# Two bias units moved behind the second half step's scores, and first-layer weight operations entered in the engine sharing

## The chip, the cores and the metric

The program runs on one core of one Trainium2 chip. The metric is the device time of an execution in microseconds; the kernel before takes 644.47 us (median of 3 runs, 644.24 to 644.6).

## The reference

An attention layer with a computed bias feeds two gated feed-forward layers, all float32:

```python
scores = scale * np.matmul(q, k.transpose(0, 1, 3, 2))          # B 2, H 8, S 576, D 64
x = (log1p(abs(i - j)) / log1p(max(i, 1)))[..., None]
bias = np.maximum(x @ w1 + b1, 0.0) @ w2                        # 32 hidden, 8 heads
attn = softmax(scores + bias)
x = np.matmul(attn, v)                                          # 1152 tokens, 512 wide
x = (x @ w_a) * (x @ w_b) @ w_out                               # 512 -> 1536 -> 512
x = (silu(x @ w_gate) * (x @ w_val)) @ w_out2
```

## The kernel before

Attention is done in half steps. A step is one pair of heads and one tile of rows; the first four steps (`t` 4) have one half each, the other sixteen have two (one per batch), 36 halves in all. The main loop (line 474) runs a pipeline over them: iteration i issues `first(i)` (scores on the tensor engine PE into the one PSUM tile `ps`, then, on the vector engine DVE, two row minima with the bias added, line 339, and, on the scalar engine ACT, two exponentials, line 345), `second(i - 1)` (nine transposes of the exponentials `es` on PE in three groups, each into a PSUM bank `tp` that is copied out as `ee`, lines 350 and 352) and `third(i - 2)` (values: `pu` from `ee` and `vv`). Every second half (and each of the first four) also transposes the inverse sums `rw` and copies them out as `rc`. There is one `ps` tile, so the scores of a half start after the minima of the half before; there are three `tp` banks, so a group of transposes waits until an earlier bank has been copied out.

The bias is made in between, in 36 units of 16 rows. `passes(u)` computes four tiles `hd` (lines 154 on DVE, 156 on ACT; eight buffers, two units' worth), and `products(u)` multiplies them on PE into one or two `tp` banks, copies these out scaled as `bt` (lines 160 and 162, the widths tell the units apart: unit 5 is 496 wide, 6 is 480, 7 is 464, 8 is 448, 9 is 432) and writes `bt` to DRAM (`bias_d`, on SP's queue). The rows of a step are read back from there by POOL's queue; those of half 4, the first of tile 0, need units 0 to 7. Four units are made ahead of the loop (`FIRST`), the rest in numbers given by `MADE`: 8 in iteration 0, 2 and 1 in turn after it. In iteration 0 the scores stand behind the fifth of these eight (`SCORED`), the minima behind the eighth, and those minima are held in program order on DVE.

PE's matmuls are all held in program order (line 100 is the helper `Pinned`, which records them; all of them have its line). What is not held is ordered by a scheduler. Work that either engine can do (`hd`, `bt`, `ee`, `rc`, `qa`, `ka`) is given to the one with less work so far, by two running sums, `share.spent`, for DVE and ACT: `on_dve` adds a linear cost in the width and picks the smaller sum. From iteration 22 on, one operation an iteration of preparing the first layer's weights (lines 270 to 274, 284, 285: twelve operations of 1024 columns, nine on DVE, three on ACT) is issued beside attention; these were not entered in the sums.

The layers after attention are bound by PE's matmuls and are not touched.

Of the kernel before, what the change touches and what calls it, by code (L numbers as in the profile page):

```python
# [32 lines left out]

UNITS = (*range(32, 36), *range(32))
FIRST = 4
MADE = (8, *(2, 1) * 8)
SCORED = 4
HDS, BTS, EES = 8, 6, 4

# [12 lines left out]
@with_exitstack  # L52
def attention_moe_moe(ctx: ExitStack, tc: tile.TileContext, qd, kd, vd, cst, lm, wm1, wm2, out):
    dram = ctx.enter_context(tc.tile_pool(name="dram", bufs=1, space=DRAM))
    bias_d = [dram.tile([P if t < 4 else 64, H, BW], F32, name=f"bias_d{t}") for t in range(5)]
    wpa = ctx.enter_context(tc.tile_pool(name="wpa", bufs=1))
    ident = wpa.tile([P, P], F32, name="ident")
    make_identity(tc.nc, ident)
    xpool = ctx.enter_context(tc.tile_pool(name="xpool", bufs=1))
    weights = Weights(tc, (wm1, wm2))  # L60
    x = Activations(xpool)

    with (
        tc.tile_pool(name="prep", bufs=2) as prep,
        tc.tile_pool(name="a4", bufs=3) as a4,
    ):
        share = Share()
        bias = ExitStack()
        staged = bias.enter_context(tc.tile_pool(name="staged", bufs=1, side="right"))
        heads = Heads(tc, prep, staged, qd, kd, vd, share)  # L70
        units = Bias(tc, bias, cst, lm, bias_d, heads, share)
        attention(ctx, tc, a4, heads, share, bias, units, bias_d, x, weights, ident)
    moe(tc, x, weights, out)
# [228 lines left out]
def attention(ctx, tc, a4, heads, share, bias, units, bias_d, x, weights, ident):  # L302
# [3 lines left out]
    with (  # L306
# [6 lines left out]
        def bias_rows(p, t, n):  # L313
            e = bias_d[t][:, 2 * p]
            return bass.AP(tensor=e.tensor, offset=e.offset + 15, ap=[[16 * H * BW, n // 16], [H * BW - 1, 16], [1, BW + S]])

        def scores(p, q, blocks, bt, sums):

            ka, kb = heads.got["k", p]
            qa, qb = q  # L320
            ps = ps2.tile([P, 2, 2, 512], F32, tag="big", name="ps")
            es = a4.tile([P, 2, S], F32, tag="es", name="es", bufs=3)
            for hf in range(2):
                for m, (lt, rt) in enumerate(((qa, ka), (qa, kb), (qb, ka))):
                    for j in range(2):
                        r = slice(64 * j, 64 * j + 64)
                        for n, (c0, b) in enumerate(blocks):
                            k0 = S * b + 288 * hf
                            pe.matmul(
                                ps[:, j, hf, :288], lt[r, c0 : c0 + P], rt[r, k0 : k0 + 288], start=m + n == 0, stop=m + n == len(blocks) + 1  # L330
                            )
            return ps, es, bt, sums

        def exponentials(ps, es, bt, sums, pinned):

            for j in range(2):
                nm = a4.tile([P, 1], F32, tag="nm", name="nm", bufs=4)
                least = (units.dve if pinned else nc.vector).tensor_tensor_reduce
                least(  # L339
                    out=es[:, j].rearrange("p (a j) -> p a j", a=2), in0=ps[:, j, :, :288], in1=bt[j].rearrange("p (a j) -> p a j", a=2),  # L340
                    op0=ALU.add, op1=ALU.min, scale=-0.125, scalar=3.0e38, accum_out=nm,
                )
                share.dve(S, 1.3)
                share.act(S, 190.0)
                nc.scalar.activation(es[:, j], es[:, j], AF.Exp, bias=nm, scale=-1.0, accum_out=sums[:, j : j + 1])  # L345
            return es.rearrange("p h k -> p (h k)")
# [81 lines left out]
        def first(i):  # L428

            idx, p, t, b = halves[i]  # L430
            if b == 0:
                bt = a4.tile([P, BW + S], F32, tag="bias", name="bt", bufs=3)
                for r in range(1 if t < 4 else B):
                    n = P if t < 4 else 64
                    heads.queue.dma_start(bt[n * r : n * r + n], bias_rows(p, t, n))
                bt = [bt[:, BW * j : BW * j + S] for j in range(2)]
                if 0 < idx < 3:
                    heads.load_v(idx + 1, nc.sync)
                    heads.split_k(idx + 1)
                if 6 <= idx + 2 < len(steps):  # L440
                    heads.fetch_q(*steps[idx + 2])
                cells[idx] = bt, a2.tile([P, 4 if t < 4 else 2], F32, tag=f"sums{t < 4}", name="sums", bufs=3)
            bt, sums = cells[idx]
            blocks = [(P * b, b)] if t < 4 else [(64 * r, r) for r in range(B)]
            for made in range(MADE[0] if i == 0 else 1):
                if i == 0:
                    units.products(*units.passes(rest.pop(0)), bank)
                if made == SCORED * (i == 0):
                    live[i] = scores(p, heads.got["q", p, t], blocks, bt, sums[:, 2 * b : 2 * b + 2])
            live[i] = exponentials(*live[i], i == 0)  # L450
            if idx == 2:
                heads.split_q(*steps[4])
            if 4 <= idx < len(steps) - 1 and b == 0:
                heads.split_q(*steps[idx + 1])

        def second(i):

            idx, p, t, b = halves[i]
            live[i] = transposed(live[i])
            if t == 4 or b == 1:  # L460
                cells["rc", idx] = inverses(place(t)[1], cells.pop(idx)[1])

        def third(i):

            idx, p, t, b = halves[i]
            if b == 0:
                cells["pu", idx] = ps0.tile([P, 512], F32, tag="pu", name="pu")
            pu = cells["pu", idx]
            blocks = [(slice(0, P), b, P * b)] if t < 4 else [(slice(64 * r, 64 * r + 64), r, 64 * r) for r in range(B)]
            values(p, pu, live.pop(i), blocks)  # L470
            if t == 4 or b == 1:
                finish(p, *place(t), cells.pop(("pu", idx)), cells.pop(("rc", idx)))

        for i in range(len(halves) + 2):
            todo = [units.passes(rest.pop(0)) for _ in range(MADE[i] if 0 < i < len(MADE) else 0)]
            if i < len(halves):
                first(i)
            if 0 <= i - 1 < len(halves):
                second(i - 1)
            if i >= 2:  # L480
                third(i - 2)
            for unit in todo:
                units.products(*unit, bank)
            if i == len(MADE) - 1:
                bias.close()
                weights.pool = weights.pools[0] = ctx.enter_context(tc.tile_pool(name="wpa2", bufs=1, side="right"))
                weights.fetch(0, 0, 0)
                weights.fetch(0, 0, 1)
                ahead = chain(weights.words(0, 0, 0), weights.split(0, 0, 0), weights.words(0, 0, 1))
            if i > len(MADE) + 4:  # L490
                for op in islice(ahead, 1):
                    units.tc.keep_in_program_order(op)


def place(t):
# [227 lines left out]
```

## Time and profile before

| | |
|---|---|
| median of 3 runs | 644.47 us (644.24 to 644.6) |
| the profiled execution | 645.35 us, its span 643.5 us |
| busy share of the span | PE 94%, DVE 83%, ACT 54%, POOL 7% |
| attention (to the first matmul of the first layer) | 0 to 200.17 us |
| mean granted TensorE clock | 0.995 |

The span runs from the first to the last instruction; the execution's time lies 1.85 us above it. The granted clock of PE is given as a share of 2.4 GHz; 0.5 is 1.2 GHz. A timeline row gives start, duration, engine, line, operation, the tiles, and in brackets the idle time of the engine before it and what ended that.

### The profile page before, as it was taken

To read this page: it belongs to the slowest core of one execution; us is meant where nothing else is said; L and a number is where in the kernel's file an instruction comes from. 1 tells how busy PE (TensorE), PEld (TensorE's weight loads), DVE (VectorE), ACT (ScalarE), POOL (GpSimd) and SP (SyncE) were. 2 spreads that over 40 slices of the span, in tenths; PEclk is the share of its full clock that TensorE was granted. 3 is DMA by queue.
4 is the path that set the end of the run, shared out by engine and by line. 5 is a ranking of instruction groups with operands and counts; after the bars stand their busy time and mean duration, and the time that the engine had idled before them with its cause. 6 is when DMAs were issued, how large, how long until landed. Compare 5 with 4: busy or idle time off the path is not lost.

```text
span 643.5 us, 11334 instructions
## 1 busy us (share of the span) xinstructions
PE 606.4 (94%) x4470; PEld 553.4 (86%) x4470; DVE 535.0 (83%) x1034; ACT 346.2 (54%) x673; POOL 45.6 (7%) x66
## 2 busy tenths in 40 slices
PE   4689898999899989999999999999989999999997
PEld 2266565688778989999999999899989999999997
DVE  6968779788988899998988979988898979896452
ACT  7878878788875464435434332455545444433110
POOL 3311110111100000000000000630000000000000
PEclk9989989999999999999999999999999999999999
DMA  9985535494512333232313131111131313100012
GB/s 344 272 232 166 178 123 157 152 226 111 156 24 69 133 114 125 81 123 85 113 66 130 66 132 66 65 66 66 65 132 66 130 66 131 66 1 1 1 49 99
DMA packets 20996, 71.56 MB, mean 111 GB/s; under 512 B 5744, under 2 KB 7424, under 8 KB 16336
## 3 DMA queue, kind: packets, MB, share of 16 engines
q1 hardware_dynamic: 12528, 52.61, 23.2%
q0 software_dynamic: 8272, 18.13, 10.7%
q8 instruction: 35, 0.57, 0.4%
q14 instruction: 17, 0.14, 0.1%
q10 hardware_dynamic: 144, 0.11, 0.1%
HBM read 57.57 MB, written 13.25 MB: 110 GB/s over the span
## 4 chain that ended last, share of the span: by engine, by line
PE 70%; DVE 17%; ACT 9%; issue 3%; DMA 1%; POOL 0%; ACTq 0%; DVEq 0%; POOLq 0%
PE po L100 20%; PE pv L100 12%; PE pb L100 10%; PE pa L100 7%; PE tp L100 7%; PE pd L100 6%; PE pu L100 5%; PE ps L100 3%; ACT hd L156 2%; ACT es L345 2%; DVE m L274 2%; DVE m L273 2%; ACT bt L162 2%; ACT ee L352 1%; DVE es L339 1%
## 5 line engine op out<-in xcount | busy, mean ns | idle before, releaser
L100 PE MATMUL po<-gh,woh 128*128 128x384 f32 x288 | 96.8, 336 | 1.4 <-DVE acc L599 1.3
L100 PE MATMUL po<-gl,woh 128*128 128x384 f32 x288 | 96.4, 335 | 1.2 <-DVE gl L534 1.2
L100 PE MATMUL po<-gh,wol 128*128 128x384 f32 x288 | 96.5, 335 | 0.0
L533 ACT CAST gh<-g 128x384 fp32r<-128x384 f32 x72 | 35.9, 514 | 88.5 <-DVE g L531 88.4
L345 ACT ACTIVATE es<-es,nm 128x576 f32<-128x576 f32 x72 | 55.7, 777 | 3.9 <-DVE nm L339 3.5
L100 PEld LDWEIGHTS po<-gh,woh 128*128 128x128 f32 x288 | 54.1, 188 | 2.4 <-DVE acc L599 2.4
L100 PEld LDWEIGHTS po<-gl,woh 128*128 128x128 f32 x288 | 54.1, 188 | 1.6 <-DVE gl L534 1.6
L100 PE MATMUL tp<-ident,es 128*128 128x128 f32 x324 | 46.7, 283 | 8.0 <-ACT ee L352 4.5
L100 PEld LDWEIGHTS po<-gh,wol 128*128 128x128 f32 x288 | 54.1, 188 | 0.0
L339 DVE CUSTOM_DVE_ANT_0 es<-ps,bt 128x576 f32<-128x576 f32 x70 | 50.0, 753 | 2.9 <-PE ps L100 2.3
L100 PE MATMUL pv<-x2h,wh 128*128 128x384 f32 x152 | 50.9, 335 | 0.0
L100 PE MATMUL pv<-x2l,wh 128*128 128x384 f32 x152 | 50.9, 335 | 0.0
L100 PE MATMUL pv<-x2h,wl 128*128 128x384 f32 x152 | 50.9, 335 | 0.0
L100 PEld LDWEIGHTS tp<-ident,es 128*128 128x128 f32 x324 | 34.6, 141 | 17.6 <-ACT ee L352 5.9
L100 PE MATMUL pu<-ee,vv 128*64 128x128 f32 (+1 forms) x800 | 48.4, 271 | 0.0
L100 PE MATMUL tp<-hd,cs 128*32 128x264 f32 (+17 forms) x352 | 36.7, 495 | 11.8 <-DVE hd L154 6.0
L270 ACT ACTIVATE m<-raw 128x1024 f32<-128x1024 f32 x36 | 41.5, 1154 | 9.5 <-DVE wl L285 4.2
L284 ACT CAST wh<-m 128x1024 fp32r<-128x1024 f32 x24 | 25.3, 1054 | 37.3 <-PE pd L100 30.0
L100 PEld LDWEIGHTS pu<-ee,vv 128*64 128x64 f32 x800 | 40.2, 139 | 5.9 <-issue 5.3
L273 DVE SCALAR_TENSOR_TENSOR m<-raw,m 128x1024 uint32<-128x1024 uint32 x36 | 44.6, 1238 | 0.2
L274 DVE SCALAR_TENSOR_TENSOR m<-raw,m 128x1024 uint32<-128x1024 uint32 x36 | 44.5, 1237 | 0.1
L534 DVE TENSOR_TENSOR gl<-g,gh 128x384 fp32r<-128x384 f32 x72 | 38.9, 552 | 5.1 <-ACT gh L533 5.0
(148 smaller groups left out, 1522.5 us busy)
## 6 DMA issues: line engine op xcount, KB each, us to landing
raw<-in_wm SPq DMA_DIRECT2D x36, 1024.0 KB, 4.8
bias_d<-bt SPq DMA_DIRECT2D x36, 295.5 KB, 4.4
bt<-bias_d POOLq DMA_DIRECT2D x16, 583.5 KB, 7.3
bt<-bias_d POOLq DMA_DIRECT2D x8, 291.8 KB, 9.7
kr<-in_kd POOLq DMA_DIRECT2D x4, 576.0 KB, 6.8
out_t<-acc SPq DMA_DIRECT2D x12, 192.0 KB, 1.9
rawq<-in_qd POOLq DMA_DIRECT2D x16, 128.0 KB, 3.7
vv<-in_vd SPq DMA_DIRECT2D x2, 640.0 KB, 5.9
```

Source lines behind the costliest of these rows:

```text
L100: return self.tc.keep_in_program_order(getattr(self.engine, name)(*args, **kwargs))
L156: self.nc.scalar.activation(dst, self.LW[:, :n], AF.Relu, bias=self.bp[:, m : m + 1])
L162: self.nc.scalar.activation(dst, src, AF.Copy, scale=self.RE[:, u : u + 1])
L270: yield nc.scalar.activation(m, hi.bitcast(F32), AF.Abs)
L273: yield nc.vector.scalar_tensor_tensor(t, lo, 29, t, op0=ALU.logical_shift_right, op1=ALU.bitwise_or)
L274: yield nc.vector.scalar_tensor_tensor(t, hi, 0xC0000000, t, op0=ALU.bitwise_and, op1=ALU.bitwise_or)
L284: yield nc.scalar.copy(wh[:, :4], mt)
L339: least(out=es[:, j].rearrange("p (a j) -> p a j", a=2), in0=ps[:, j, :, :288], in1=bt[j].rearrange("p (a j) -> p a j", a=2), op0=ALU.add, ...
L345: nc.scalar.activation(es[:, j], es[:, j], AF.Exp, bias=nm, scale=-1.0, accum_out=sums[:, j : j + 1])
L352: nc.scalar.copy(dst, src)
L533: nc.scalar.copy(gh, g)
L534: nc.vector.tensor_tensor(gl, g, gh.bitcast(F32), op=ALU.subtract)
```

## The change

`MADE` becomes 6, 4, 1 and then 2 and 1 in turn. Two of the eight units ahead of the first minima (units 6 and 7) go to iteration 1, which now makes four; of those, the two first have their products issued between `first(1)` and `second(0)`, that is behind the second half's scores and ahead of the first half's transposes. After iteration 1 the same ten units have been made as before. And each weight operation issued beside attention now adds 1150 to the sum of its engine.

```diff
-MADE = (8, *(2, 1) * 8)
+MADE = (6, 4, 1, *(2, 1) * 7)
...
             todo = [units.passes(rest.pop(0)) for _ in range(MADE[i] if 0 < i < len(MADE) else 0)]
             if i < len(halves):
                 first(i)
+            if i == 1:
+                for _ in range(2):
+                    units.products(*todo.pop(0), bank)
             if 0 <= i - 1 < len(halves):
                 second(i - 1)
...
             if i > len(MADE) + 4:
                 for op in islice(ahead, 1):
                     units.tc.keep_in_program_order(op)
+                    share.spent[op.ins.engine == mybir.EngineType.Activation] += 1150.0
```

On PE the place is the second half's scores (`ps`, six groups of four matmuls) and the first half's transposes (`ident,es`); the `tp<-hd,cs` rows are the units' products. Of before and change:

```order
 L100 MATMUL tp<-hd,cs 32x496 x4
-L100 MATMUL tp<-hd,cs 32x480 x4
-L100 MATMUL tp<-hd,cs 32x464 x4
 L100 MATMUL ps<-ka,qa 128x288 x4
 L100 MATMUL ps<-kb,qa 128x288 x4
```

```order
 L100 MATMUL ps<-kb,qa 128x288 x4
 L100 MATMUL ps<-ka,qb 128x288 x4
+L100 MATMUL tp<-hd,cs 32x480 x4
+L100 MATMUL tp<-hd,cs 32x464 x4
 L100 MATMUL tp<-ident,es 128x128 x9
 L100 MATMUL tp<-ident,rw 128x128
```

Units 6 and 7 go from ahead of the second scores to behind them; nothing else on PE moves.

On ACT the place is from the second half's exponentials (of tile `es_460` before, `es_442` in the change) to the copies of the first half's transposes. Before:

```order
L345 ACTIVATE es_351,sums_240<-es_351,nm_430 128x576
L383 COPY rw_510<-rs_507 128x128
L352 COPY ee_491<-tp_492 128x384
L345 ACTIVATE es_460,sums_458<-es_460,nm_485 128x576
L352 COPY ee_491<-tp_497 128x384
L345 ACTIVATE es_460,sums_458<-es_460,nm_488 128x576
L383 COPY rw_607<-rs_604 128x128
```

Now:

```order
L345 ACTIVATE es_442,sums_440<-es_442,nm_467 128x576
L345 ACTIVATE es_442,sums_440<-es_442,nm_470 128x576
L156 ACTIVATE hd_415<-LW_94,bp_100 128x448
L156 ACTIVATE hd_419<-LW_94,bp_100 128x448
L162 ACTIVATE bt_473<-tp_474,cs_93 128x480
L162 ACTIVATE bt_473<-tp_474,cs_93 128x111
L156 ACTIVATE hd_425<-LW_94,bp_100 128x432
L156 ACTIVATE hd_429<-LW_94,bp_100 128x432
L162 ACTIVATE bt_482<-tp_483,cs_93 128x464
L162 ACTIVATE bt_482<-tp_483,cs_93 128x127
L352 COPY ee_491<-tp_492 128x384
L352 COPY ee_491<-tp_502 128x384
```

Both units' copies out of PSUM (`tp_474`, `tp_483`) are on ACT, behind the second half's exponentials and ahead of the copies `ee` of the first half's transposes; the second of the three groups of transposes reuses the bank of `tp_474`, and the `rw` transpose that of `tp_483`.

On DVE the place is in iteration 32, around the weight operation of line 273. Before:

```order
L272 TENSOR_SCALAR m<-m 128x1024
L339 ISA es,nm<-ps,bt 128x576
L339 ISA nm 128x1
L339 ISA es,nm<-ps,bt 128x576
L339 ISA nm 128x1
L210 CAST qa<-rawq 128x256
L350 COPY ee<-tp 128x384
L390 COPY rc<-tp 128x256
L273 SCALAR_TENSOR_TENSOR m<-raw,m 128x1024
L214 TENSOR_TENSOR qb<-rawq,qa 128x256
L339 ISA es,nm<-ps,bt 128x576
```

Now:

```order
L272 TENSOR_SCALAR m<-m 128x1024
L339 ISA es,nm<-ps,bt 128x576
L339 ISA nm 128x1
L339 ISA es,nm<-ps,bt 128x576
L339 ISA nm 128x1
L273 SCALAR_TENSOR_TENSOR m<-raw,m 128x1024
L214 TENSOR_TENSOR qb<-rawq,qa 128x256
L339 ISA es,nm<-ps,bt 128x576
```

Three small operations that stood on DVE between the minima are on ACT. Over the last fourteen halves DVE has 15 of the copies `ee` and `rc` where it had 22; ACT has the seven.

## Rows read from the trace of the kernel before

**Rows 1.** The page's head and its first part, busy time of each engine.

```profile
span 643.5 us, 11334 instructions
PE 606.4 (94%) x4470; PEld 553.4 (86%) x4470; DVE 535.0 (83%) x1034; ACT 346.2 (54%) x673; POOL 45.6 (7%) x66
```

**Rows 2.** Windows of 2 us: length, engines, PEclk (granted clock), DMA, GB/s.

```profile
32.00:34.00 2.00, 0.41 (x4) 0.44 (x6) 1.80 (x6) 1.57 (x4) 0.26 (x1) 0.94 1.06 364
34.00:36.00 2.00, 2.00 (x21) 2.00 (x19) 0.34 (x2) 0.72 (x3) 0.93 (x2) 0.50 1.08 322
...
88.00:90.00 2.00, 2.00 (x17) 1.61 (x18) 1.32 (x4) 1.70 (x5) 0.58 (x1) 0.59 0.67 217
```

**Rows 3.** Timeline of PE around the second half's scores and the two halves after.

```profile
33.59 0.75 PE L100 MATMUL ps<-ka,qa 64*128 64x288 f32 x4 [3.78 <-DVE nm L100]
...
36.67 1.42 PE L100 MATMUL tp<-ident,es 128*128 128x128 f32 x9
...
40.74 0.53 PE L100 MATMUL ps<-ka,qa 64*128 64x288 f32 x4
...
42.54 0.88 PE L100 MATMUL tp<-ident,es 128*128 128x128 f32 x6
...
44.46 1.39 PE L100 MATMUL pu<-ee,vv 128*64 128x64 f32 x40
```

**Rows 4.** Timeline of DVE: minima of halves 0, 2 and 4, and what precedes.

```profile
29.34 0.81 DVE L154 TENSOR_SCALAR hd<-LW,bp 128x448 f32<-128x448 f32 x2
...
32.01 0.75 DVE L100 CUSTOM_DVE_ANT_0 es<-ps,bt 128x576 f32<-128x576 f32 x1
...
43.26 0.75 DVE L339 CUSTOM_DVE_ANT_0 es<-ps,bt 128x576 f32<-128x576 f32 x1
...
53.80 0.75 DVE L339 CUSTOM_DVE_ANT_0 es<-ps,bt 128x576 f32<-128x576 f32 x1
```

**Rows 5.** ACT: an exponential, by the page's groups, and three timeline rows.

```profile
L345 ACT ACTIVATE es<-es,nm 128x576 f32<-128x576 f32 x72 | 55.7, 777 | 3.9 <-DVE nm L339 3.5
...
32.12 0.37 ACT L162 ACTIVATE bt<-tp,cs 128x127 f32<-128x127 f32 x1 [0.96 <-DVE bt L160]
...
41.08 0.62 ACT L162 ACTIVATE bt<-tp,cs 128x448 f32<-128x448 f32 x1
41.59 1.67 ACT L156 ACTIVATE hd<-LW,bp 128x416 f32<-128x416 f32 x3
```

**Rows 6.** Timeline of PE: transposes that waited, with no scores behind them yet.

```profile
55.63 0.55 PE L100 MATMUL tp<-ident,es 128*128 128x128 f32 x3 [1.15 <-ACT ee L352]
...
87.85 0.55 PE L100 MATMUL tp<-ident,es 128*128 128x128 f32 x3 [0.99 <-ACT ee L352]
```

**Rows 7.** POOL's wait for half 4's bias, and DMA issues of 40.5:46.

```profile
39.91 0.59 POOL L100 DMA_DIRECT2D bt<-bias_d  x1 [4.98 <-DMA bias_d<-bt]
...
bt<-bias_d POOLq DMA_DIRECT2D x2, 583.5 KB, 7.6
```

**Rows 8.** Windows from value matmul to value matmul, two halves each.

```profile
137.55:145.52 7.97, 7.16 (x86) 5.92 (x85) 6.49 (x19) 6.81 (x17) 1.17 (x2) 1.00 1.00 226
...
152.59:159.66 7.07, 7.07 (x85) 5.91 (x84) 7.04 (x22) 5.92 (x16) 1.17 (x2) 1.00 0.39 100
159.66:168.07 8.41, 7.25 (x85) 5.95 (x84) 8.38 (x25) 6.95 (x18) 1.17 (x2) 1.00 0.70 219
168.07:175.83 7.76, 7.18 (x85) 5.93 (x85) 6.97 (x20) 6.71 (x17) 0.58 (x1) 1.00 0.37 92
...
182.90:190.78 7.88, 7.23 (x86) 5.94 (x85) 7.20 (x19) 5.56 (x14) 0.00 (x0) 1.00 0.01 2
```

**Rows 9.** Timelines around the weight operations: PE, ACT, DVE.

```profile
167.71 0.44 PE L100 MATMUL tp<-ident,rw 128*128 128x128 f32 x2 [1.01 <-ACT ee L352]
...
165.93 1.04 ACT L284 CAST wh<-m 128x1024 fp32r<-128x1024 f32 x1
...
184.75 1.22 DVE L273 SCALAR_TENSOR_TENSOR m<-raw,m 128x1024 uint32<-128x1024 uint32 x1
```

## Prediction

> **What bounds the kernel now.** The page first: PE is busy 94% of the span and every other engine is below it [rows 1], so time is to be gained only where PE idles or runs slowly. Cutting the span into windows shows where that is. From the first layer on PE is all but full; attention, the first 200 us, holds nearly all the idle time. Two stretches of it concern this change.
>
> The first is the start. The timeline of PE shows 3.78 us of idle time in front of the second half's scores, ended by the minima of the first half; the scores then take from 33.59 to 36.67, 3.08 us, where the next half's take from 40.74 to 42.54, 1.80 us [rows 3]. The windows give the reason: the granted clock is 0.50 of 2.4 GHz, so 1.2 GHz, from 34 to 36 [rows 2]. The stall thus costs its own length and 1.3 us more. What the minima waited for is read from DVE: from 29.34 to 32.01 it is occupied with work for units 6 to 9 [rows 4].
>
> The second is the end of attention, where weight operations run beside it. An undisturbed pair of halves takes 7.07 us; four pairs take longer, by 0.90, 1.34, 0.69 and 0.81 us, 3.74 in all [rows 8]. In the second of them PE waits 1.01 us for an ACT copy standing behind a 1.04 us cast of the weights; in the fourth a 1.22 us DVE operation stands in front of the minima [rows 9].
>
> **The change part by part.** *Ahead of the first minima.* The 2.67 us of DVE work from 29.34 to 32.01 go behind the minima; one more `hd` of unit 7 comes in front of them, 0.41 us by the pair at 29.34 [rows 4]. The minima start at 32.01 - 2.67 + 0.41 = 29.75, and the second scores, which followed them by 1.58 us (33.59 - 32.01), at 31.33: 2.26 us earlier. The casts `ka` of the last two head pairs swap engines; I take 0 for that, within 0.5 either way, since DVE and ACT are both full there.
>
> *Clock of the second scores.* PE no longer has the products of units 6 and 7 in front of them, so its idle time does not shrink by 2.26: its start moves forward as well. Two units cost PE some 1.6 us (an estimate: the 4.07 us from 36.67 to 40.74 less nine transposes, 1.42, and about 1 us of waiting [rows 3]), so it idles at least 3.78 - 2.26 + 1.6 = 3.1 us. The clock fell behind 3.78 us of idle time, and near 88 us behind a 0.99 us wait among short pieces of work [rows 2, 6]. I take the low clock again: the scores end at 31.33 + 3.08 = 34.4. At the full clock it would be 33.1; that end goes into the range.
>
> *What now stands behind them.* The first minimum's result comes 0.7 us later (35.1); ACT then runs its list as the order shows it: two exponentials of 0.78, two `hd` of 0.55, the copies of unit 6 (0.55 and 0.25, between the rows of 0.62 and 0.37), two `hd`, the copies of unit 7 [rows 5]. That is 1.55 + 1.1 + 0.8 + 1.1 + 0.8 = 5.35 us, to 40.45. Before, these copies were over by 32.5 [rows 5]. The transposes of the first half, which followed the scores at once, now wait bank by bank for these copies, and the products of units 8 and 9 come behind them; these and the `rw` transpose need some 2.0 us more, so the third scores start at 42.45 instead of 40.74: **+1.7 us**. The gain of 2.26 us is spent before it reaches the third scores.
>
> *How much of that stays.* Two halves on, PE waited 1.15 us for a copy on a full ACT [rows 6]. ACT's list up to there is a little shorter now (two `ee` copies fewer, one `hd` more), so this wait shrinks as PE comes later; I let it take 0.9. The start then costs **+0.8 us**; its ends are -0.5 (full clock, 1.3 less) and +2.5 (low clock at the third scores too, 1.7 more).
>
> *SP and POOL.* No DMA is added. The write of unit 7 is issued at about 40.5 instead of 32.5. Before, POOL's read of half 4's bias was released at 39.91, 7.4 us after the last copy, and it lands 7.6 us after its issue [rows 5, 7]: now 40.45 + 7.4 + 7.6 = 55.45. The minima that need it ran at 53.80 [rows 4], now between 54.6 and 55.5. I take 0; the other end is +1.7, as much again as the start's own delay at the third scores. The `q` fetches behind that read on POOL have slack of a whole step, and cost nothing while it lands in time.
>
> *Sharing at the end.* Seven copies of 0.4 to 0.55 us leave DVE. The fourth pair gains most: `qa`, `ee` and `rc`, some 0.9 us, go from in front of the weight operation and so from in front of the minima; I take 0.7 of its 0.81. In the second, two of DVE's operations delayed scores by 0.3 in all, which goes too. The waits for ACT (the first pair, the 1.01 of the second, the third) stay: the order there still has the weight operation ahead of the first copy. **-1.0 us**, between 0 (the copies merely move the queue to ACT) and -2.0.
>
> *Between them* `hd` and `ee` are dealt out anew over some 90 us, with PE waiting about 1 us in most steps [rows 6]. No row says which way this goes: 0, within 1 either way; the dip near 88 us belongs to it.
>
> The sum is +0.8 + 0 - 1.0 + 0 = -0.2 us on the profiled execution's 645.35, 645.15. That execution lies 0.88 above the median of the runs, so I forecast **644.3 us**: no change that can be measured. About 0.2%, 1.3 us, is what a measurement of this kernel tells from none; faster means under 643.2, slower over 645.8.
>
> **Rivals.** *Faster: the stall is really gone.* If PE keeps the full clock for the second scores, all behind them comes 1.3 us earlier (start -0.5), and if relief at the end reaches one of the ACT waits as well (-1.5), it is -2.0: 642.5 us. For it: DVE's cause of the stall does go, and 3.1 us is less than 3.78. Against it: a much shorter wait had the same result near 88 us.
>
> *Slower: the idle time moves behind the second scores.* From about 36.0 (34.4 and the products of units 6 and 7) PE has only three short groups of transposes until 40.45, each behind a copy. If the clock falls there as near 88 us [rows 2, 6], the products of units 8 and 9 and the third scores run at 1.2 GHz, 1.7 us longer: start +2.5, sum +1.5, 646.0 us. It decides where PE's gaps ahead of 40.45 exceed those ahead of 87.85, the wait of 0.99 us and what lies before it; I count some 3 us of them. The Trainium skill, page "TensorE: Matmul & The Clock Gate", section "A second HAM failure mode: psum-queue depth-cycling", says of this pattern that a PE which steps through PSUM banks with small pauses swings between its two clock levels and loses throughput in each burst. By that rule it would be this rival; the trace agrees near 88 us, and shows other waits of about 1 us at the full clock.
>
> *Slower: the bias of half 4 is late.* If write and read need 1.7 us more than the rows say, on queues that others use, half 4's minima wait that long: sum +1.5, 646.0 us. Against it: the 7.4 us were read while the DMA engines were full, 1.06 in the window from 32 to 34 [rows 2].
>
> *The sharing does nothing*, since three of the four waits name ACT: without its -1.0 it is 645.3 us, inside the forecast's band and counted with it.
>
> **How the numbers follow.** The forecast 0.40, from 643.2 to 645.8; the faster rival 0.36; the low clock behind the second scores 0.16; late bias 0.08. So 0.36 faster, 0.40 the same, 0.24 slower. The range must reach both sides: down to 642.0, half a microsecond beyond the faster rival, and up to 646.3, a little beyond the slower ones; some 0.1 is left out on each side.
>
> **What would show it.** Right: first minima near 29.8 and second scores near 31.3 at a clock of 0.5; unit 7's copies on ACT ending past 40; third scores near 42.5; the fourth late pair near 7.2 us, the first and third as before. Wrong: third scores before 41 (the copies are not in the way), or after 43.5 with a clock of 0.5 around 42; a DMA ending DVE's wait at half 4; or a pair in the middle of attention that differs by over 1 us, which this working has no term for.

## The result, and the profile after

The changed kernel takes 649.67 us (median of 6 runs, 647.92 to 650.47), the kernel before beside it 644.54: a ratio of 1.0072, with a 95% interval from 1.0059 to 1.0085. It is slower by 0.7%, where no change was forecast. The profiled execution takes 649.1 us, 3.75 more than that of before [rows 1]; PE's share stays at 94%, and DVE is busy 3 us less:

```profile
span 647.3 us, 11339 instructions
...
PE 607.6 (94%) x4470; PEld 552.7 (85%) x4470; DVE 532.0 (82%) x1029; ACT 347.7 (54%) x678; POOL 45.9 (7%) x66
```

(First minima, second and third scores are those of halves 0, 1 and 2, as in the prediction.) Where the time went is seen by setting the starts of the same work side by side: the first value matmul (`pu`) of a half step in PE's timeline, and the first matmul of the first layer.

| value matmuls of half | before, us | after, us | later by |
|---|---|---|---|
| 0 | 44.46 | 50.03 | 5.57 |
| 4 | 66.89 | 71.63 | 4.74 |
| 7 | 81.78 | 86.72 | 4.94 |
| 9 | 94.40 | 97.57 | 3.17 |
| 16 | 130.48 | 134.30 | 3.82 |
| first layer | 200.17 | 203.97 | 3.80 |

The net loss arises before half 0's values, at the start. PE's timeline there answers to [rows 3]:

```profile
25.70 1.04 PE L100 MATMUL tp<-hd,cs 128*32 128x496 f32 x8
33.95 0.85 PE L100 MATMUL ps<-ka,qa 64*128 64x288 f32 x4 [7.20 <-DVE nm L100]
...
37.13 2.88 PE L100 MATMUL tp<-hd,cs 128*32 128x480 f32 x16
39.94 0.55 PE L100 MATMUL tp<-ident,es 128*128 128x128 f32 x3
41.62 0.55 PE L100 MATMUL tp<-ident,es 128*128 128x128 f32 x3 [1.14 <-ACT bt L162]
42.82 0.90 PE L100 MATMUL tp<-ident,es 128*128 128x128 f32 x3 [0.65 <-DVE ee L350]
43.51 0.46 PE L100 MATMUL tp<-ident,rw 128*128 128x128 f32 x1
43.90 2.80 PE L100 MATMUL tp<-hd,cs 128*32 128x448 f32 x16
46.63 0.54 PE L100 MATMUL ps<-ka,qa 64*128 64x288 f32 x4
...
50.03 1.39 PE L100 MATMUL pu<-ee,vv 128*64 128x64 f32 x40
```

The second scores, forecast for 31.33, start at 33.95, 0.36 later than before. PE's idle time in front of them has not shrunk but grown, from 3.78 to 7.20 us: its own work left the gap and the gap's end stayed. From there to the third scores it is 12.68 us, before 7.15. DVE's timeline, answering to [rows 4], names what held the first minima:

```profile
29.26 0.73 DVE L160 TENSOR_SCALAR bt<-tp,cs 128x496 f32<-128x496 f32 x1
29.91 0.45 DVE L154 TENSOR_SCALAR hd<-LW,bp 128x464 f32<-128x464 f32 x1
32.35 0.76 DVE L100 CUSTOM_DVE_ANT_0 es<-ps,bt 128x576 f32<-128x576 f32 x1 [2.00 <-DMA bt<-bias_d]
```

DVE is free at 30.35, as the change meant it to be, and then waits 2.00 us for a DMA: the read of the first step's bias. The chain that ended last, in order of time (start, length, what), shows the second of the two reads:

```profile
21.57 0.65 POOL bt L100
22.21 10.00 DMA bt<-bias_d
...
32.35 0.76 DVE es L100
```

It was to be had from the trace of before. POOL's timeline there (first fence) and the DMA issues between 21.3 and 21.8 us (second) say:

```profile
21.00 1.30 POOL L100 DMA_DIRECT2D bt<-bias_d  x2 [1.75 <-DMA bias_d<-bt]
```

```profile
bt<-bias_d POOLq DMA_DIRECT2D x2, 291.8 KB, 9.7
```

The second issue begins near 21.65 and lands 9.7 us later, near 31.35: 0.66 us before DVE was done at 32.01 [rows 4]. A wait that ended that little earlier shows nowhere as a wait.

The windows (granted clock is the third number from the end), answering to [rows 2]:

```profile
30.00:32.00 2.00, 0.00 (x0) 0.00 (x0) 0.36 (x1) 0.34 (x1) 0.00 (x0) 0.50 1.02 207
...
34.00:36.00 2.00, 2.00 (x16) 2.00 (x18) 0.34 (x2) 1.08 (x4) 1.19 (x2) 0.50 0.73 230
...
40.00:42.00 2.00, 0.86 (x8) 0.56 (x6) 0.83 (x3) 2.00 (x5) 0.00 (x0) 1.00 0.26 70
...
44.00:46.00 2.00, 2.00 (x12) 0.49 (x16) 0.65 (x3) 0.75 (x3) 0.00 (x0) 0.50 0.42 160
...
88.00:90.00 2.00, 2.00 (x28) 1.12 (x28) 1.78 (x7) 2.00 (x6) 0.49 (x1) 1.00 0.26 38
```

The clock is at 1.2 GHz from the idle time on, comes back, and falls a second time behind the transposes that waited 1.14 and 0.65 us. There the products of units 8 and 9 take 2.80 us. The dip of the kernel before near 88 us is missing, which is most of the 1.77 us between halves 7 and 9 in the table (its price is read below, at `before_warm1`). ACT's copies of units 6 and 7 stand where the order had put them, answering to [rows 5]:

```profile
40.69 0.88 ACT L162 ACTIVATE bt<-tp,cs 128x480 f32<-128x480 f32 x2
...
42.55 0.89 ACT L162 ACTIVATE bt<-tp,cs 128x464 f32<-128x464 f32 x2
```

The end of attention, windows as in [rows 8] (second, third and fourth late pair, and the stretch behind them), and that last stretch in the kernel before:

```profile
163.69:171.90 8.21, 7.23 (x85) 5.91 (x84) 7.96 (x25) 7.18 (x19) 1.17 (x2) 1.00 0.63 213
171.90:180.02 8.12, 7.17 (x85) 5.93 (x84) 6.58 (x20) 6.78 (x17) 0.58 (x1) 1.00 0.40 101
...
187.12:194.21 7.09, 7.09 (x86) 5.93 (x85) 6.35 (x16) 6.51 (x18) 0.00 (x0) 1.00 0.01 3
194.21:201.63 7.42, 6.40 (x73) 5.08 (x72) 5.53 (x16) 6.13 (x16) 0.00 (x0) 1.00 0.42 141
```

```profile
190.78:197.83 7.05, 6.46 (x73) 5.08 (x72) 5.91 (x17) 5.51 (x15) 0.00 (x0) 1.00 0.42 150
```

The fourth pair fell from 7.88 to 7.09, the second from 8.41 to 8.21; the third rose from 7.76 to 8.12 and the last stretch from 7.05 to 7.42. From half 18's values to the first layer it is 62.60 us, before 62.62.

### The profile page after: what moved, and what is told of

Its sections match the earlier page's. It is cut to its first block, busy times and chain, and to the rows that moved or that the text cites. A ratio compares the mean times of both kernels' runs of the same rounds, so it can differ in the third digit from the quotient of the medians.

```text
span 647.3 us, 11339 instructions
## 1 busy us (share of the span) xinstructions
PE 607.6 (94%) x4470; PEld 552.7 (85%) x4470; DVE 532.0 (82%) x1029; ACT 347.7 (54%) x678; POOL 45.9 (7%) x66
## 4 chain that ended last, share of the span: by engine, by line
PE 70%; DVE 15%; ACT 7%; DMA 3%; issue 3%; POOL 0%; ACTq 0%; DVEq 0%; POOLq 0%
PE po L100 20%; PE pv L100 12%; PE pb L100 10%; PE pa L100 7%; PE tp L100 7%; PE pd L100 6%; PE pu L100 5%; PE ps L100 4%; ACT es L345 2%; DVE m L274 2%; DMA bt<-bias_d 2%; DVE m L273 2%; ACT ee L352 1%; DVE g L535 1%; DMA kr<-in_kd 1%
## 6 DMA issues: line engine op xcount, KB each, us to landing
bt<-bias_d POOLq DMA_DIRECT2D x8, 291.8 KB, 10.0
```

## The experiments

Six kernels start from the kernel before. Eight have the moved units without the change's second part: `units_only` and seven that start from it. Each ratio is to the kernel before on the same chip, with its 95% interval.

**The two parts apart.** `units_only` is the change without

```diff
-                    share.spent[op.ins.engine == mybir.EngineType.Activation] += 1150.0
```

> The change without its second part: the two units moved, weight operations not entered in the sums. If the start alone makes the loss (theory): 649.5 us, within 0.6; its start reads as in the change, the third scores near 46.6, and its pairs late in attention as in the kernel before (the fourth near 7.9 us instead of the change's 7.1). If the sharing has a part in the loss (rival): under 648.5 us.

650.59 us, ratio 1.0090 (1.0065 to 1.0115), a little more than expected; second scores 34.15, third 46.81. So the moved units make the loss, not the sharing. But they don't make all of it at the start: from half 18's values to the first layer it takes 63.37 us, where the kernel before takes 62.62, the second late pair 8.88 instead of 8.41, the last stretch 7.43 instead of 7.05. In that pair `qa`, `ee` and `rc` now stand on DVE ahead of the weight operation of line 274 (166.29), and that ahead of the next minima. PE waits twice for minima, the second time behind that operation; in the kernel before it waits for none there:

```profile
165.43 0.40 PE L100 MATMUL ps<-ka,qa 64*128 64x288 f32 x2 [0.32 <-DVE nm L339]
...
169.34 0.40 PE L100 MATMUL ps<-ka,qa 64*128 64x288 f32 x2 [0.48 <-DVE nm L339]
```

Moving units changes the running sums, and so which engine gets what 100 us later. The forecast had no term for this. All eight kernels with the moved units alone show it, 63.30 to 63.37 us. `share_only` is the kernel before with that line alone added:

> The kernel before with weight operations entered in the sums, no unit moved. If the sharing only moves waits from one late pair to the next (theory): 644.5 us, within 0.5, with the fourth pair near 7.1 us and the pairs around it longer by as much together. If it gains what was forecast: 643.5. If it is a part of the loss: over 645.5.

643.58 us, ratio 0.9983 (0.9968 to 0.9997). Its windows for the second and third late pair, the fourth, and the last stretch:

```profile
158.46:166.43 7.97, 7.25 (x86) 5.93 (x85) 7.62 (x24) 7.47 (x20) 1.17 (x2) 1.00 0.70 226
166.43:174.53 8.10, 7.17 (x85) 5.93 (x84) 6.57 (x20) 6.76 (x17) 0.58 (x1) 1.00 0.37 101
...
181.63:188.73 7.10, 7.10 (x86) 5.93 (x85) 6.36 (x16) 6.52 (x18) 0.00 (x0) 1.00 0.01 3
188.73:196.16 7.43, 6.40 (x73) 5.08 (x72) 5.53 (x16) 6.13 (x16) 0.00 (x0) 1.00 0.43 141
```

Against before: -0.44, +0.34, -0.78, +0.38, in all -0.5. The gains are those forecast, but the copies given to ACT bring waits for ACT elsewhere, which the forecast had at nothing. The profile puts the part, on the kernel before, at 0.43 us (1.24 us ahead of before at half 18, 1.67 at the first layer), half of what was forecast. On top of the moved units it is worth 0.77 (63.37 to 62.60), which is what those had cost there. The median's 1.58 us is more than that; this profile has no dip near 88 us either, though nothing is changed there, so the median alone doesn't size the part.

**What holds the first minima.** `units_nobias0` leaves out the first step's read, so its result is not that of the reference:

```diff
-                for r in range(1 if t < 4 else B):
+                for r in range(0 if idx == 0 else 1 if t < 4 else B):
-                bt = [bt[:, BW * j : BW * j + S] for j in range(2)]
+                bt = [bt[:, BW * j : BW * j + S] if idx else units.LW for j in range(2)]
```

> The two units moved, as in the first run, and the first step's bias is left out: no read of it, its minima take another tile that has long been there. If the landing of that read is what held the first minima (theory): they start at 29.9 instead of 32.35, the second scores at 31.5, after some 4.8 us of idle PE, and the time falls by 2.4 us, to 647.1 (within 0.8). If something else on DVE or PE held them (rival): they stay near 32.3 and the time stays at 649.5.

648.67 us, ratio 1.0059 (1.0037 to 1.0081). DVE's timeline, and PE's:

```profile
30.42 0.75 DVE L100 CUSTOM_DVE_ANT_0 es<-ps,LW 128x576 f32<-128x576 f32 x1
```

```profile
32.00 0.85 PE L100 MATMUL ps<-ka,qa 64*128 64x288 f32 x4 [5.35 <-DVE nm L100]
```

The wait is gone, and the second scores come 2.15 us earlier than in `units_only`; the time falls by 1.9, less than the 2.4 expected. The read held the minima. It also shows that the read is not the larger part: without it the moved units still lose 0.6%, and from second to third scores it is still 12.58 us.

Why does each of the two reads of 292 KB take some 10 us? `units_k3` puts the read of the fourth pair's keys behind it on POOL's queue:

```diff
-            heads.fetch_k(p + 2)
+            if p == 0:
+                heads.fetch_k(2)
...
+                if idx == 0:
+                    heads.fetch_k(3)
```

> The two units moved, and the read of the fourth pair's keys (576 KB, issued at 18.3) put behind the read of the first step's bias on POOL's queue. If traffic beside it is what makes the bias read take 10 us (theory): it lands some 1.5 us earlier, the first minima start near 30.9 instead of 32.4 and the second scores near 32.5. If it is the number of its pieces or the write before it (rival): within 0.5 of 32.4. The split of those keys comes later on ACT and DVE in either case.

653.73 us, ratio 1.0127 (1.0102 to 1.0152). Issued at 21.53, the two reads took 10.6 us, where those of `units_only`, issued at 22.40, took 9.4. The keys' read, issued at 23.35, took 13.7 us, so it ran beside them all the same. The minima, in DVE's timeline, started later, not earlier:

```profile
33.37 0.76 DVE L100 CUSTOM_DVE_ANT_0 es<-ps,bt 128x576 f32<-128x576 f32 x1 [3.99 <-DMA bt<-bias_d]
```

`units_hold` holds the next steps' reads back, by a copy of `nm` on POOL's queue ahead of them:

```diff
+                live["nm"] = nm
...
+                if idx == 1:
+                    heads.queue.tensor_copy(a2.tile([P, 1], F32, tag="held", name="held", bufs=1), live.pop("nm"))
```

> The two units moved, and the reads of the second and later steps' bias held on POOL's queue until the first half's minima are done. If the four reads behind it share the DMA engines with the first step's read and so make it take 10 us (theory): it lands several us earlier and the first minima start at 30.4, as in the run without that bias. If not (rival): they stay within 0.7 of 32.5. The second half, whose bias is then late, pays in either case, so the total says nothing.

Its one run takes 659.54 us, since the second step's bias is then late, as expected. POOL's DMA issues between 20 and 23 us, where only two of the six reads are left, and DVE's timeline:

```profile
bt<-bias_d POOLq DMA_DIRECT2D x2, 291.8 KB, 9.9
```

```profile
32.77 0.76 DVE L100 CUSTOM_DVE_ANT_0 es<-ps,bt 128x576 f32<-128x576 f32 x1 [2.11 <-DMA bt<-bias_d]
```

The reads behind don't make it slow: that theory fell. Putting the keys behind didn't help, but doesn't clear them, since they then ran beside the bias for longer. The units' own writes, which run at that time on SP's queue, were not held. Whether the writes, the keys or the read's own pieces set the 10 us stays open.

**What the moved work costs behind the second scores.** `units_warm` fills PE's idle time:

```diff
+            if i == 1:
+                spare = bank()
+                for _ in range(44):
+                    pe.transpose(spare[:, :P], ident, ident)
```

> The two units moved, and 44 transposes of the identity put into PE's idle time ahead of the second scores, whose result nobody reads. The first minima should stay at 32.3. If the long idle time costs through the clock (theory): second scores start at 34.0 with a clock of 1.0 and take 1.8 instead of 3.2 us, the products of the moved units 1.4 instead of 2.8, those of the next two 1.4 instead of 2.8; the third scores come some 3 us earlier, near 43.6 instead of 46.6, and the time falls to 646.5 (within 0.8). If the copies on ACT ahead of the transposes set the third scores (rival): they come at most 1.4 us earlier, and the time stays over 648.

650.16 us, ratio 1.0103 (1.0063 to 1.0142): no gain. PE's timeline, and two windows:

```profile
34.02 0.54 PE L100 MATMUL ps<-ka,qa 64*128 64x288 f32 x4 [2.39 <-DVE nm L100]
...
39.67 0.55 PE L100 MATMUL tp<-ident,es 128*128 128x128 f32 x3 [1.59 <-ACT bt L162]
```

```profile
34.00:36.00 2.00, 1.98 (x28) 1.81 (x32) 0.41 (x3) 1.16 (x5) 1.19 (x2) 1.00 0.75 239
...
42.00:44.00 2.00, 1.69 (x9) 0.58 (x13) 0.29 (x1) 1.20 (x5) 0.00 (x0) 0.50 0.52 197
```

The scores ran at 2.4 GHz, as expected. But the transposes then waited longer for ACT's copies (1.59 instead of 1.16 in `units_only`), the clock fell behind those waits, and the third scores came at 45.81: of the 3 us expected, 1.0. The rival was right. It is also what the forecast's slower rival had described: idle time that moves behind the second scores. The Trainium skill, page "TensorE: Matmul & The Clock Gate", section "A second HAM failure mode: psum-queue depth-cycling", was named for it there: a PE that steps through PSUM banks with small pauses swings between its clock levels. The window from 42 to 44 agrees, with 0.50.

`units_warm_dve` adds to this a change in `scaled`, which gives the copies of the two units to DVE:

```diff
-        if self.share.on_dve(n):
+        if u in (6, 7):
+            self.share.dve(n)
+        if u in (6, 7) or self.share.on_dve(n):
```

> The two units moved, PE's idle time filled as in the run with 44 transposes, and the copies of the two moved units forced onto DVE. If those copies, behind the exponentials on ACT, are what held the transposes and brought the clock down behind them (theory): no wait of the transposes for a copy of a unit, the clock at 1.0 up to the third scores, which start near 42.3 instead of 45.8, and the time falls by 3 us or more, to 646.5 (within 1.0). If the mere order, two units' products ahead of the transposes, sets it (rival): third scores after 44.5 and over 648.5 us.

647.66 us, ratio 1.0047 (1.0026 to 1.0068); third scores at 44.88. In between: 0.9 us earlier than in `units_warm`, and a better median, but the third scores are where the rival had them. The clock did not hold this time, as PE's timeline and a window show:

```profile
34.31 0.54 PE L100 MATMUL ps<-ka,qa 64*128 64x288 f32 x4 [2.11 <-DVE nm L100]
```

```profile
36.00:38.00 2.00, 2.00 (x16) 0.92 (x17) 1.10 (x3) 0.00 (x0) 0.00 (x0) 0.50 0.66 156
```

`units_behind` puts the products behind the transposes, from `units_only` without

```diff
-            if i == 1:
-                for _ in range(2):
-                    units.products(*todo.pop(0), bank)
```

> The two units moved as in the change, but with their products behind the first half's transposes instead of ahead of them; weight operations not entered. If the place ahead of the transposes is what costs, by copies that hold the banks (theory): transposes follow the second scores at once, no wait for a copy of a unit among them, third scores near 45.0 instead of 46.8, and 649.0 us. If any place behind the second scores costs as much, since four units' products and their hidden tiles follow each other at the low clock (rival): third scores near 46.8 or later and 650.5 us.

648.73 us, ratio 1.0071 (1.0057 to 1.0086), as the theory had it; second scores 33.68, third 44.75. No transposes wait for a unit's copy. Now the units wait, in PE's timeline:

```profile
39.34 3.63 PE L100 MATMUL tp<-hd,cs 128*32 128x480 f32 x24 [0.80 <-ACT ee L352]
43.89 0.93 PE L100 MATMUL tp<-hd,cs 128*32 128x432 f32 x8 [0.91 <-ACT bt L162]
```

From second to third scores it is 11.07 us here, against 7.15 in the kernel before and 12.66 in `units_only`. So of the 5.5 us by which `units_only` is longer there, 3.9 are the two units' work, in the better of the two places behind the scores, and 1.6 the place ahead of the transposes, with its waits and its second low clock. `units_behind_warm`, the same with the 44 transposes, was to take the clock out of this:

> The two units moved, their products behind the first transposes, and 44 transposes of the identity in the idle time ahead of the second scores. If the moved units' own work behind the second scores costs some 3 us whatever the clock (theory): second scores near 33.9 at a clock of 1.0, third scores 4 to 5 us later than in the kernel before with its idle time filled (38.5), so 42.5 to 43.5, and 646 us (within 1.0). If the loss is nearly all clock (rival): third scores within 2 us of 38.5 and under 643.5 us.

647.88 us, ratio 1.0034 (1.0016 to 1.0052), inconclusive. In its profile the bias landed later still, the minima started at 33.56, 3.27 us of idle time were left and the clock fell all the same; from second to third scores it was 11.2 us.

**The other direction.** `before_warm` is the kernel before with the filling, 22 transposes instead of 44:

> The kernel before, with 22 transposes of the identity in the 3.8 us of idle time ahead of the second scores. If the idle time's cost beyond its length is the clock (theory): the second scores start at 33.6 as before, take 1.8 instead of 3.1 us, the third ones start 1.3 us earlier, near 39.4, and the time is 643.5 where the kernel before takes 644.8. If later waits take it up (rival): third scores earlier, the value matmuls of the fifth half not, and the same time as before.

641.16 us (640.71 to 642.25), ratio 0.9938 (0.9918 to 0.9958): more than expected, and the fastest kernel of the study. PE's timeline, and a window:

```profile
33.60 0.54 PE L100 MATMUL ps<-ka,qa 64*128 64x288 f32 x4 [0.68 <-DVE nm L100]
...
38.51 0.53 PE L100 MATMUL ps<-ka,qa 64*128 64x288 f32 x4
```

```profile
34.00:36.00 2.00, 2.00 (x29) 1.84 (x27) 0.83 (x3) 0.85 (x4) 1.04 (x2) 1.00 0.96 312
```

The second scores start where they did, at twice the clock; the third come 2.23 us earlier, since the transposes and products behind them run faster too. All of it is kept: half 16's values start 3.87 us earlier, 2.3 of them from here and the rest from the missing dip near 88 us. In all six runs the granted clock is 0.999 or 1.000 (0.995 to 0.997 for the kernel before), so the dip was in none; that this is the filling's doing is not shown. `before_warm1` is its control, with `range(1)`:

> A control for the filling: the same spare bank, with one transpose in it instead of 22. If the work in the idle time keeps the clock and so makes the gain (theory): no gain with one, 644.5 us, the second scores at a clock of 0.5 taking 3.1 us. If the further bank or the place of the transposes makes it (rival): about 641.2 us, as with 22.

644.48 us, ratio 1.0001 (0.9988 to 1.0013): it is the filling, not the bank. PE waited 2.95 us and the clock fell during the scores. Two windows of this profile also bear on the dip near 88 us:

```profile
86.00:88.00 2.00, 0.72 (x5) 0.31 (x3) 2.00 (x7) 2.00 (x6) 0.00 (x0) 1.00 0.68 210
88.00:90.00 2.00, 1.82 (x25) 1.58 (x25) 1.65 (x5) 2.00 (x6) 0.58 (x1) 1.00 0.70 213
```

PE is idle for 1.28 us of the first window, as it waits near there in the kernel before [rows 6]; the order of the work is the same; and the clock stays, where it fell there [rows 2]. So the order of the work does not fix the dip: it comes in one profile and not in another. From half 7 to half 9 this profile gains 1.58 us on that of before: that is its price.

`early8` moves one unit the opposite way, unit 8's products ahead of the second scores:

```diff
+            if i == 1:
+                for _ in range(1):
+                    units.products(*todo.pop(0), bank)
             if i < len(halves):
                 first(i)
```

> The kernel before, with the products of one unit (448 wide) taken from behind the first transposes and put ahead of the second scores, into PE's idle time: the opposite direction to the change. If the idle time is free for PE's work and shorter idle time keeps the clock (theory): second scores at 33.6 at a clock of 1.0, third ones 2.0 us earlier, near 38.7, and 643.0 us. If the unit's copies then hold the minima or the banks (rival): second scores after 34.2, and the time as before or longer.

644.53 us, ratio 0.9991 (0.9975 to 1.0008), no gain. The bias was later than DVE again, and with 2.77 us of idle time left the clock fell. DVE's timeline:

```profile
32.79 0.76 DVE L100 CUSTOM_DVE_ANT_0 es<-ps,bt 128x576 f32<-128x576 f32 x1 [0.58 <-DMA bt<-bias_d]
```

`early8_warm` adds 16 transposes behind that unit:

> The kernel before, with one more unit's products (448 wide) ahead of the second scores and 16 transposes of the identity behind them. If PE's idle time there is free for a unit's work, once the clock is kept (theory): second scores at 33.6 to 34.3 at a clock of 1.0, 0.9 us of products less behind the transposes, third scores near 38.0, and 640.6 us, against 641.2 with the filling alone. If the bias read, landing later than DVE's work ends, or the unit's copies take it back (rival): 641.2 or more.

642.98 us, ratio 0.9957 (0.9939 to 0.9975). The clock held, and the third scores came at 38.34, 0.17 us before those of `before_warm` although the second had started 0.59 later; half 0's values gain 0.56 us on `before_warm`. At half 10 they are 1.45 behind it: 1.43 us go between halves 6 and 7, where the clock falls once more (0.50 in the window from 76 to 78, 1.00 in `before_warm`), and 1.07 between halves 9 and 10. Work is dealt out differently there; that this brings the fall is not shown. `share_warm`, both things that helped:

> The kernel before with both of what helped so far: weight operations entered in the sums, and 22 transposes of the identity ahead of the second scores. If the two gains lie in different stretches and add up (theory): second scores at a clock of 1.0, the late pairs as in the run with the sums alone, and 0.4 us less than with the transposes alone: 640.8 us. If an earlier start only meets later waits (rival): 641.2 or more.

641.84 us, ratio 0.9961 (0.9948 to 0.9975). Its profile shows the two gains in their two stretches (the late one 0.47 us from half 18 to the first layer), but 641.84 us is no less than `before_warm` alone, so that they add up is not shown. The filling is what is shown to help.

## Why the prediction was wrong

- *Ahead of the first minima.* This is the step that failed: "The minima start at 32.01 - 2.67 + 0.41 = 29.75" counted DVE's list alone. They need the bias too, whose landing, near 31.35 in the trace of before, would have capped the gain at 0.66 us; in the change it landed at 32.2 and left none. Measured 32.35; second scores 2.62 us later than forecast. `units_nobias0` shows it.
- *Clock of the second scores.* Right: 0.5. The idle time behind which it fell was 7.20 us, not 3.1: the minima came 2.62 us later than forecast, and PE ran out of work at 26.75 instead of 29.81, 3.06 earlier, where 1.6 had been counted.
- *What stands behind them.* The order was read rightly; ACT's copies came at the place and in the order given. Third scores 46.63 instead of 42.45: 2.62 us are the step above. The other 1.56 are for the most part the second low clock, which had been priced at 1.7 as a rival and given 0.16: from the third group of transposes to the third scores it is 3.81 us, in `units_warm_dve`, at the full clock there, 2.79. This was a second mistake of the forecast, and doesn't hang on the first: in `units_nobias0` the minima came early, and the clock fell there too (0.60 in the window from 42 to 44).
- *How much stays.* Right in size: 0.9 us were to be absorbed, and the loss goes from 5.57 at half 0 to 4.74 at half 4. The start so cost 4.74 where +0.8 was forecast.
- *SP and POOL.* Right in outcome, by luck. Half 4's read was issued at 47.36 and landed 9.1 us later, at 56.46, where 55.45 was forecast; minima at 55.5 would have waited for it. They started at 60.21, without a wait, since the whole start was late.
- *Sharing.* Forecast -1.0; in the change the late stretch is 0.02 us shorter than before. On the kernel before the part gives -0.43 (`share_only`) and -0.47 (`share_warm`): the fourth pair was right (7.09 against 7.2), but that the waits for ACT stay was wrong, since they grew, by 0.36 us in the third pair and 0.37 in the last stretch. And the moved units cost 0.75 there (`units_only`), which the forecast had at nothing; the part gave that back and no more.
- *Between them.* Forecast 0 within 1: from half 4 to half 16 it was -0.92. That is luck: the missing dip alone is worth 1.58, and without it this would have been a loss of 0.66.

Added up, the profiled execution was to take 645.15 us and took 649.1: 3.9 more at the start, 1.0 more in the late stretch, 0.9 less in between. The range, up to 646.3, failed because its slower rivals were each priced alone, on top of minima that were taken to come early.

## What to carry to other kernels

Before work is taken away in front of an instruction, look up when each of its other inputs arrives, DMAs above all: the trace names only the wait that ended last, and the next one may end 0.7 us earlier. Work that fills a gap which something else ends can be free there; moved out, it cost this kernel 3.9 us up to the third scores in one place and 5.5 in the other. If such a gap must stay, work of no use in it can pay: 22 transposes whose result nobody reads made this kernel 0.6% faster. And where a running sum deals out work, a change at one end can move waits at the other, here 0.75 us some 100 us later.

## What was not expected of the hardware

The same length of idle time did not always have the same result: the clock held behind 2.39 us (`units_warm`) and 0.68 us (`before_warm`), and fell behind 2.11 (`units_warm_dve`), 2.77 (`early8`) and 2.95 us (`before_warm1`). In `early8` it had fallen by the time the scores began, in the other two it fell within them. And the first step's reads of 291.8 KB, 64 rows each, took from 7.6 (`units_behind`) to 11.4 us (`units_behind_warm`) to land, while the 576 KB read of keys, issued at 18.2 in the kernel before, took 6.2.
